# An FFT filter followed by a maxout layer: loads of the opening held behind the first exchange, filter copies and weights on the ACT queue, exchange reads in two t halves, four products on GpSimd

## The chip, the cores and the metric

The kernel runs on one core of one Trainium2 chip. The metric is the device time of one execution in microseconds (us). Every kernel below was run several times. A run counts as slow when its granted TensorE clock (the share of the full clock that the chip allows) is far below the others' or its time is over 1.5% above that kernel's fastest. All medians and ratios below are of fast runs.

Engines in the profile: PE is TensorE (matmul), PEld its weight loads, DVE is VectorE, ACT is ScalarE, POOL is GpSimd, SP is SyncE, which here does nothing but issue DMAs. A trailing q, as in SPq, marks an engine's DMA issues. Such an issue takes place in order: if the next DMA of SP has to wait for data, all DMAs of SP behind it wait too.

## The reference

```python
def _attn_ref(x, filt_r, filt_i):           # x: 8 x 3072 x 256, filters: 1537 x 256
    X = np.fft.rfft(x, axis=1)
    Y = X * (filt_r + 1j * filt_i)[None, :, :]
    return np.fft.irfft(Y, n=x.shape[1], axis=1)

def _moe_ref(x, w1, w2, w_out):             # x: 24576 x 256, hidden size 1024
    return np.maximum(x @ w1, x @ w2) @ w_out
```

The output is the second function of the first one's result, in float32.

## The kernel before

The transform of length 3072 = 128 x 24 is done as two small transforms by matmul, with an exchange through DRAM between them, and the inverse in the same way. For one of the eight batches:

- `gen_f1`: `x` times `C1` gives `at`, stored to DRAM as `ad`, read back rearranged as `bt` (the first exchange).
- `gen_f2`: sixteen groups `g` of two values of `t` each: `px` = `U` times `bt`, one product `pqt` with the filter `F`, then `pz`, stored to DRAM as `zd` and read back rearranged as `zr` (the second exchange).
- `s4`: `py` = `zr` times `G1`; then the maxout layer (`ph`, `po`) in six tiles of 512 tokens, each with one store of output.

```python
# gen_f1, after the last store of ad
for h in range(2):
    for rs in range(4):
        src = ad[32 * rs + 16 * h:32 * rs + 16 * h + 16].rearrange("t n d -> n t d")
        nc.sync.dma_start(out=bt_[24 * rs:24 * rs + 24, 16 * h:16 * h + 16], in_=src)

# gen_f2
def s3(g, pqt):
    ...                                     # pz by four matmuls, zt <- pz on ACT
    if g % 2 == 1:
        nc.sync.dma_start(out=zd[:, 2 * g - 2:2 * g + 2], in_=zt)

for g in list(range(2, 16)) + [0, 1]:
    ...                                     # px by two matmuls
    V.tensor_tensor(pqt, px..., F[:, :, 2 * g:2 * g + 2], OP.mult)
    pend.append((g, pqt))
    if len(pend) > 1:
        s3(*pend.pop(0))
    yield
s3(*pend.pop(0))
zr_ = zrpool.tile([128, N2, D], BF16, tag="zr")
for c in range(3):
    for rs in range(4):
        src = zd[24 * rs + 8 * c:24 * rs + 8 * c + 8].rearrange("n t d -> t n d")
        nc.sync.dma_start(out=zr_[32 * rs:32 * rs + 32, 8 * c:8 * c + 8], in_=src)

# s4, tile i of the batch: four of the 24 columns of zr, all 128 partitions
TE.matmul(py[:, n], zr[b][:, 4 * i + n, 128 * dc:128 * dc + 128], G1, ...)

# the opening
table_c(); load_f(1, 16); load_f(16, 32); uu, mk = tables_u()
drain(gen_f1(0))
copy_f(1, 16); copy_f(16, 32)               # F partitions 48..95 <- 0..47, on SP
load_f0(); load_w()                         # 16 small loads; 2 weights on SP, Wo on Pool
for c in range(12): load_x(1, c)
sines_u(uu, mk); tables_pe()
...                                         # f2 of batch 0, with fix_f before product 14
prep_w(); drain(f2); drain(gen_f1(1)); s4(0)
```

After that one loop interleaves, step by step, the maxout layer of batch b with `gen_f2` of batch b+1 and `gen_f1` of batch b+2.

## Time and profile before

| | before |
|---|---|
| time at the outset, median of 3 runs | 615.84 us (615.23 to 616.15) |
| span of the profiled run | 613.5 us |
| first product `pqt` starts | 55.3 us |
| sixteenth product ends | 82.0 us |
| first `ph` of the maxout layer | 111.7 us |
| first output store | 130.2 us |
| from output store 12 to 18, 18 to 24 and so on (one batch) | 62.7 us |

From the page: the busy time of each engine, then the main DMA queue (packets, MB, share of 16 engines' time).

```profile
PE 536.0 (87%) x4008; PEld 395.0 (64%) x4008; DVE 335.0 (55%) x430; ACT 329.5 (54%) x588; POOL 86.0 (14%) x167
...
q1 hardware_dynamic: 66720, 54.17, 33.6%
```

The next view gives busy time in chosen stretches; the last three columns are the granted TensorE clock, the mean busy share of the DMA engines and what they moved.

```profile
core 0: us, PE busy (x) PEld busy (x) DVE busy (x) ACT busy (x) POOL busy (x), PEclk, DMA share, GB/s
26.00:46.00 20.00, 4.79 (x35) 3.25 (x33) 4.00 (x7) 3.57 (x8) 6.34 (x12) 1.00 1.16 183
234.00:242.00 8.00, 8.00 (x64) 5.69 (x63) 3.25 (x5) 3.92 (x7) 0.54 (x1) 1.00 0.94 260
200.00:300.00 100.00, 100.00 (x784) 75.21 (x783) 61.23 (x73) 61.73 (x111) 14.96 (x28) 1.00 0.71 178
```

From 200 to 300 us TensorE is busy in all of the 100 us. A microsecond taken from another engine is worth nothing there. In the opening (26 to 46 us) it is busy 4.8 of 20 us, while the DMA engines are full. So nearly all the time that can be won lies before about 120 us (a wait of 3.4 us in the second batch, shown below, is the exception).

The timeline of the events that this document follows (start, length, engine and line, output<-input, count; in brackets the idle time before and what ended it):

```profile
27.10 16.50 SPq L318 DMA_DIRECT2D bt__271<-ad  x8
43.72 7.84 SPq L102 DMA_DIRECT2D F<-F  x4
55.27 2.35 DVE L346 TENSOR_TENSOR pqt<-px,F 96x1024 bf16<-96x1024 f32 x2 [23.51 <-DMA F<-F]
76.68 3.02 ACT L335 ACTIVATE zt<-pz 96x512 bf16<-96x512 f32 x6 [11.65 <-DMA zd<-zt]
93.45 10.04 SPq L357 DMA_DIRECT2D zr__665<-zd  x12
108.08 3.05 ACT L310 ACTIVATE at<-pa 128x512 bf16<-128x512 f32 x6 [14.38 <-DMA ad<-at]
...
232.91 7.05 SPq L357 DMA_DIRECT2D zr__2222<-zd  x12
239.89 0.61 PE L369 MATMUL py<-G_59,zr__2222 128*128 128x128 bf16 x8
```

Read it as three waits of the opening: the first product waits for the filter copy, ACT waits 11.6 us for a `zd` store that stands behind small loads on SP, and ACT waits 14.4 us for `ad` stores that stand behind twelve `zr` reads.

The waits of TensorE for the whole run (us in total, times, longest), those that matter here:

```profile
PE px L343 <- DMA bt__271<-ad: 15.3, 1, 15.3
PE py L369 <- ACT at L310: 14.6, 1, 14.6
...
PE px L343 <- DMA bt__1412<-ad: 3.4, 1, 3.4
```

The same view for SP between 200 and 250 us:

```profile
SPq L357 <- DMA zd<-zt: 4.7, 2, 4.2
...
SPq L318 <- DMA ad<-at: 1.7, 1, 1.7
```

### The profile page before, as it was taken

The page shows a single profiled execution, that of the slowest core. Times are in us where ns is not written, and L with a number is a line of the kernel's source. Part 1 is how long each engine was busy: PE and PEld are TensorE (multiplying, and loading weights), DVE is VectorE, ACT ScalarE, POOL GpSimd, SP SyncE. Part 2 cuts the span into 40 slices and gives each one's busy share as a digit, 9 for nine tenths or more (in the row PEclk, how much of TensorE's full clock was granted, in tenths as well). Part 3 has the DMA queues.
Part 4 walks back from the last instruction along what each step waited for, and adds up shares of the span by engine and source line. Part 5 has one row for each costly group of instructions (what it writes and reads, how often), then busy time and mean ns, then how long its engine had stood idle before and what let it go on. Part 6 is the DMA issues. An engine that isn't in the chain of part 4 may idle for free.

```text
span 613.5 us, 10246 instructions
## 1 busy us (share of the span) xinstructions
PE 536.0 (87%) x4008; PEld 395.0 (64%) x4008; DVE 335.0 (55%) x430; ACT 329.5 (54%) x588; POOL 86.0 (14%) x167
## 2 busy tenths in 40 slices
PE   3403771799979999999999999999999999999995
PEld 0203550477657777777777777777777777777774
DVE  8203740288337664666466637663667377734342
ACT  3801161566536754765476556765666455555541
POOL 8430002011111111111121102110000000000000
PEclk9999996699989999999999999999999999999998
DMA  8997529656976596658767785778336822261111
GB/s 140 208 188 148 180 62 219 171 123 169 225 182 156 134 220 198 153 152 183 212 150 179 163 218 145 183 156 233 125 112 161 225 83 78 74 185 70 69 69 69
DMA packets 90784, 94.62 MB, mean 154 GB/s; under 512 B 7360, under 2 KB 71504, under 8 KB 90592
## 3 DMA queue, kind: packets, MB, share of 16 engines
q1 hardware_dynamic: 66720, 54.17, 33.6%
q0 software_dynamic: 24016, 39.81, 28.5%
q8 instruction: 31, 0.51, 0.3%
q14 instruction: 17, 0.14, 0.1%
HBM read 56.72 MB, written 50.33 MB: 174 GB/s over the span
## 4 chain that ended last, share of the span: by engine, by line
PE 43%; issue 34%; DMA 12%; SPq 4%; POOL 3%; ACT 1%; DVE 1%; POOLq 0%; ACTq 0%
PE ph L385 14%; PE po L410 13%; PE po L405 3%; DMA xb<-in_x_dram 3%; PE pz L333 3%; PE px L343 3%; PE pz L334 3%; DMA Wo<-in_moe_w_out_dram 2%; DMA zd<-zt 2%; SPq L117 2%; POOL out_dram L416 2%; PE pa L309 2%; PE py L369 2%; DMA ad<-at 2%; DMA zr__665<-zd 1%
## 5 line engine op out<-in xcount | busy, mean ns | idle before, releaser
L410 PE MATMUL po<-Wo,gt 128*128 128x256 bf16 x1536 | 230.4, 273 | 0.0
L390 ACT ACTIVATE gt<-ph 128x512 bf16<-128x512 f32 x288 | 170.7, 593 | 100.4 <-PE ph L385 97.0
L346 DVE TENSOR_TENSOR pqt<-px,F 96x1024 bf16<-96x1024 f32 x128 | 156.0, 1219 | 107.6 <-PE px L343 83.6
L410 PEld LDWEIGHTS <-gt 128*128 128x128 bf16 x1536 | 150.2, 98 | 58.2
L335 ACT ACTIVATE zt<-pz 96x512 bf16<-96x512 f32 x128 | 75.3, 593 | 111.4 <-PE pz L334 87.9
L412 DVE COPY ot<-po 128x512 f32<-128x512 f32 x96 | 66.4, 692 | 75.8 <-PE po L410 75.8
L416 POOL DMA_DIRECT2D out_dram<-ot x48 | 25.8, 537 | 452.9 <-DVE ot L412 418.1
L385 PEld LDWEIGHTS <-Wd 128*128 128x128 bf16 x768 | 74.0, 99 | 19.5 <-issue 4.8
L310 ACT ACTIVATE at<-pa 128x512 bf16<-128x512 f32 x96 | 55.8, 597 | 54.0 <-PE pa L309 33.9
L388 DVE TENSOR_SCALAR gt<-ph 128x512 bf16<-128x512 f32 x96 | 65.5, 682 | 28.7 <-PE ph L385 28.7
L333 PE MATMUL pz<-pqt,VP 96*96 96x256 bf16 x256 | 67.9, 289 | 11.0 <-DVE pqt L346 10.7
L334 PE MATMUL pz<-pqt,VQ 96*96 96x256 bf16 x256 | 68.2, 290 | 0.0
L87 POOL DMA_DIRECT2D xb<-in_x_dram x96 | 51.4, 558 | 66.4 <-PE pa L309 50.4
L343 PEld LDWEIGHTS <-U 96*96 96x96 bf16 x256 | 32.5, 134 | 24.6 <-issue 22.9
L309 PE MATMUL pa<-xb,C_58 128*128 128x512 bf16 x96 | 38.3, 409 | 10.3 <-DMA xb<-in_x_dram 9.4
L334 PEld LDWEIGHTS <-VQ 96*96 96x96 bf16 x256 | 33.4, 130 | 13.2 <-issue 12.7
L333 PEld LDWEIGHTS <-VP 96*96 96x96 bf16 x256 | 33.7, 131 | 1.8 <-DVE pqt L346 1.1
L343 PE MATMUL px<-bt__271,U 96*96 96x256 bf16 x32 | 9.8, 416 | 18.3 <-DMA bt__271<-ad 15.3
L309 PEld LDWEIGHTS <-C_58 128*128 128x128 bf16 x96 | 9.5, 99 | 18.3 <-issue 7.5
L369 PE MATMUL py<-G_59,zr__665 128*128 128x128 bf16 x48 | 4.6, 248 | 14.6 <-ACT at L310 14.6
L369 PEld LDWEIGHTS <-zr__665 128*128 128x128 bf16 x48 | 3.9, 112 | 15.9 <-DMA zr__665<-zd 9.8
L374 DVE TENSOR_SCALAR y__760<-py 128x512 bf16<-128x512 f32 x1 | 0.7, 692 | 19.9 <-PE py L369 19.9
(334 smaller groups left out, 565.8 us busy)
## 6 DMA issues: line engine op xcount, KB each, us to landing
out_dram<-ot POOLq DMA_DIRECT2D x48, 512.0 KB, 3.9
xb<-in_x_dram POOLq DMA_DIRECT2D x96, 128.0 KB, 6.0
ad<-at SPq DMA_DIRECT2D x48, 256.0 KB
zd<-zt SPq DMA_DIRECT2D x64, 192.0 KB
bt__271<-ad SPq DMA_DIRECT2D x8, 192.0 KB
zr__665<-zd SPq DMA_DIRECT2D x12, 128.0 KB
bt__727<-ad SPq DMA_DIRECT2D x8, 192.0 KB
zr__1295<-zd SPq DMA_DIRECT2D x12, 128.0 KB
```

The source lines that it names most:

```text
L309: TE.matmul(pa, C1, xb[b, c], start=True, stop=True)
L310: S.activation(at[:, 2 * (c % 2):2 * (c % 2) + 2], pa, AF.Copy)
L333: TE.matmul(pz[:, i], VP[:, 2 * g + i], pqt[:, 0, i], start=True, stop=False)
L334: TE.matmul(pz[:, i], VQ[:, 2 * g + i], pqt[:, 1, i], start=False, stop=True)
L335: S.activation(zt[:, 2 * (g % 2):2 * (g % 2) + 2], pz, AF.Copy)
L343: TE.matmul(px[:, i], U[:, 2 * g + i].rearrange("p a b -> p (a b)"), bt_[:, 2 * g + i], start=True, stop=True)
L346: V.tensor_tensor(pqt, px.rearrange("p (o i) d -> p o i d", o=1).to_broadcast([QP, 2, 2, D]), F[:, :, 2 * g:2 * g + 2], OP.mult)
L385: TE.matmul(ph, Wd[:, dc, 128 * j:128 * j + 128], y_[:, dc].rearrange("p a b -> p (a b)"), start=(dc == 0), stop=(dc == 1))
L388: V.tensor_scalar(gt[tt][:, j], ph, 0.0, None, OP.max)
L390: S.activation(gt[tt][:, j], ph, AF.Relu)
L410: TE.matmul(p_, g_[:, jj, 128 * n:128 * n + 128], Wo[:, jj], start=False, stop=(jj == 7))
L412: V.tensor_copy(ot[tt][:, n - 1:n + 1], po[tt])
```

## The change

The intent is to shorten the opening in four ways.

1. Loads that the first product does not need (`x` of the next batch, `Wo`) are held until after products; F0 comes in four loads and a copy.
2. The filter copies and the two weight loads go from SP to the ACT queue, so they no longer stand behind the exchange reads.
3. The groups start with `t` 16 to 31, and `zr` is read in two halves of `t`: the upper half as soon as its eight groups are done, the lower one at the end. This holds for all eight batches.
4. In batch 0, Pool takes four of the sixteen products.

```diff
+    zrpool = ctx.enter_context(tc.tile_pool(name="zrpool", bufs=2))
 ... (cut: the tile pool of zr leaves its later place)
     def copy_f(t0, t1):
         for ri in range(2):
-            nc.sync.dma_start(out=F[48:96, ri, t0:t1], in_=F[0:48, ri, t0:t1])
+            S.dma_start(out=F[48:96, ri, t0:t1], in_=F[0:48, ri, t0:t1])
 ... (cut: F0 in four loads on SP, then copy_f0, two DMAs on ACT)
     def load_w():
-        nc.sync.dma_start(out=w1f, ...)
-        nc.sync.dma_start(out=w2f, ...)
+        S.dma_start(out=w1f, ...)
+        S.dma_start(out=w2f, ...)
+
+    def load_wo():
         G.dma_start(out=Wo, ...)
 ... (cut; in s3, after the store of zd)
+            if g == 15:
+                zr[b] = zrpool.tile([128, N2, D], BF16, tag="zr", name="zr")
+                read_z(1)
+            if g == 1:
+                read_z(0)
+
+        def read_z(h):
+            for rs in range(4):
+                src = zd[24 * rs:24 * rs + 24, 16 * h:16 * h + 16].rearrange("n t d -> t n d")
+                nc.sync.dma_start(out=zr[b][32 * rs + 16 * h:32 * rs + 16 * h + 16], in_=src)
-        for g in list(range(2, 16)) + [0, 1]:
+        for n, g in enumerate(list(range(8, 16)) + list(range(2, 8)) + [0, 1]):
 ...
-            V.tensor_tensor(pqt, px..., F[:, :, 2 * g:2 * g + 2], OP.mult)
+            E = V
+            if b == 0 and n in (1, 5, 9, 12):
+                E = G
+                xs = init.tile([QP, 2, D], FP32, tag="xs", name="xs")
+                S.activation(xs, px, AF.Copy)
+                px = xs
+            E.tensor_tensor(pqt, px..., F[:, :, 2 * g:2 * g + 2], OP.mult)
 ... (cut: the twelve zr reads at the end of gen_f2 go)
+    load_f0()
     table_c()
+    load_f(16, 32)
     load_f(1, 16)
-    load_f(16, 32)
     uu, mk = tables_u()
     drain(gen_f1(0))
-    copy_f(1, 16)
-    copy_f(16, 32)
-    load_f0()
-    load_w()
-    for c in range(12):
-        load_x(1, c)
     sines_u(uu, mk)
     tables_pe()
+    copy_f(16, 32)
+    copy_f(1, 16)
+    copy_f0()
+    load_w()
 ... (cut: fix_f one product later)
+        if n == 1:
+            load_wo()
+        for c in range(12):
+            if n == (1, 5, 9)[c // 4]:
+                load_x(1, c)
+    drain(f2)
     prep_w()
 ...
-    drain(f2)
     drain(gen_f1(1))
```

The loop over `h` in the `bt` reads is not touched. It still reads `t` 0 to 15 first, while the groups now begin with `t` 16.

More of the change, by code (lines that the diff above doesn't have):

```diff
@@ L109, in load_f0, with copy_f0 @@
             for dr in range(2):
-                for mm, row0 in enumerate((0, 96) if dr == 0 else (32, 64)):
-                    for q in range(2):
-                        p0 = 48 * q + 24 * dr + mm
-                        if p0 == 48:
-                            nc.sync.dma_start(out=F0[48:49, ri], in_=f[1536:1537, :])
-                            nc.sync.dma_start(out=F0[50:72:2, ri], in_=fsrc(f, 128, 128, J - 1, 1, 1))
-                        else:
-                            nc.sync.dma_start(out=F0[p0:p0 + 23:2, ri], in_=fsrc(f, row0, 128, J, 1, 1))
+                src = bass.AP(f.tensor, f.offset + 32 * dr * D, [[128 * D, J], [(96 - 64 * dr) * D, 2], [1, D]])
+                nc.sync.dma_start(out=F0[24 * dr:24 * dr + 24, ri], in_=src)
+    def copy_f0():
+        S.dma_start(out=F0[48:96], in_=F0[0:48])
+        S.dma_start(out=F0[48:49, 0], in_=filt_r[1536:1537, :])
     SW = init.tile([QP, QP], BF16)
@@ L275, in load_w @@
     def load_w():
-        nc.sync.dma_start(out=w1f, in_=moe_w1.rearrange("(c p) j -> p c j", p=128))
-        nc.sync.dma_start(out=w2f, in_=moe_w2.rearrange("(c p) j -> p c j", p=128))
+        S.dma_start(out=w1f, in_=moe_w1.rearrange("(c p) j -> p c j", p=128))
+        S.dma_start(out=w2f, in_=moe_w2.rearrange("(c p) j -> p c j", p=128))
+    def load_wo():
         G.dma_start(out=Wo, in_=moe_w_out.rearrange("(c p) j -> p c j", p=128))
@@ L345, in gen_f2 @@
             pqt = pqpool.tile([QP, 2, 2, D], BF16, tag="pq")
-            V.tensor_tensor(pqt, px.rearrange("p (o i) d -> p o i d", o=1).to_broadcast([QP, 2, 2, D]),
+            E = V
[4 more added lines that the diff above has]
+                px = xs
+            E.tensor_tensor(pqt, px.rearrange("p (o i) d -> p o i d", o=1).to_broadcast([QP, 2, 2, D]),
                             F[:, :, 2 * g:2 * g + 2], OP.mult)
@@ L352, in gen_f2 @@
         s3(*pend.pop(0))
-        zr_ = zrpool.tile([128, N2, D], BF16, tag="zr")
-        for c in range(3):
-            for rs in range(4):
-                src = zd[24 * rs + 8 * c:24 * rs + 8 * c + 8].rearrange("n t d -> t n d")
-                nc.sync.dma_start(out=zr_[32 * rs:32 * rs + 32, 8 * c:8 * c + 8], in_=src)
-        zr[b] = zr_
         yield
@@ L421, in drain @@
             pass
+    load_f0()
     table_c()
+    load_f(16, 32)
     load_f(1, 16)
-    load_f(16, 32)
     uu, mk = tables_u()
     drain(gen_f1(0))
-    copy_f(1, 16)
-    copy_f(16, 32)
-    load_f0()
-    load_w()
-    for c in range(12):
-        load_x(1, c)
     sines_u(uu, mk)
     tables_pe()
+    copy_f(16, 32)
+    copy_f(1, 16)
+    copy_f0()
+    load_w()
     f2 = gen_f2(0)
-    for g in range(16):
-        if g == 13:
+    for n in range(16):
+        if n == 14:
             fix_f()
         next(f2)
+        if n == 1:
[4 more added lines that the diff above has]
+    drain(f2)
     prep_w()
     setup.close()
-    zrpool = ctx.enter_context(tc.tile_pool(name="zrpool", bufs=2))
     ypool = ctx.enter_context(tc.tile_pool(name="ypool", bufs=3))
```

## The prediction

> **What bounds the kernel now.** Matrix work saturates TensorE from about 120 us on (20.0 of every 20 us busy in the stretch table from 200 us), so only the opening can give time back. The first maxout matmul (`ph`) starts at 111.7 us. The chain of waits up to there is mostly DMA and SP issues. The timeline gives three blocks:
>
> 1. To 55.3 us: the first product waits for the filter copy F<-F. The DMA engines are busy throughout (mostly 150 to 260 GB/s). The exchange reads `bt` are issued from 27.1 us but land at 46, because the next batch's `x` and the output weight share the engines; the filter copies leave SP only after them (43.7 to 51.6).
> 2. 55.3 to 81.9: sixteen products, one each 1.37 us (VectorE 1.22), plus a stall of about 4 us: the store of `zt` stands on SP behind 16 small issues of F0 (0.7 us each), so ACT waits 11.6 us.
> 3. 81.9 to 111.7: weight preparation (7 us) ahead of the last product, last store of `zd` at 93.2, twelve `zr` reads issued over 10 us, and ACT waiting 14.4 us for stores of `ad` held behind them.
>
> **What the change does.**
>
> Block 1: moves 2.1 MB (as written) of other loads behind the exchange, and only half of the filter copy has to be there for the first product. 9.8 MB before the first product become about 7.0; at the 190 GB/s of this stretch that is 15 us less. The `bt` reads still start near 27. First product about 40 us. [...]
>
> Block 2: the 4 us stall goes. Pool's four products I expect to cost, not to save: TensorE is in order and only one product is pending, so a Pool product holds up everything two steps on. [...] Block 2 stays near 29 us.
>
> Block 3: the last product no longer waits for weight preparation, half of `zr` is read earlier, and four reads instead of twelve stand before the `ad` stores. From 30 us to about 17.
>
> First `ph` near 86 us: 26 less, all on the critical path because TensorE is saturated afterwards. In the second batch the 3.4 us stall at 174.5 us (reads `bt` behind twelve `zr` issues) should shrink by about 2, less what it costs that products now begin with the half read last. Later batches: nothing.
>
> **Prediction.** 615.8 - 26 - 1 = 589 us; 8 in 10 between 579 and 599. Faster by over 2%: 0.95; within 2%: 0.04; slower: 0.01.
>
> **What would show each step.** The timeline: first product at 38 to 44 us instead of 55.3; `bt` landed by 40; [...] no ACT wait on `zd` over 3 us; first `ph` at 82 to 92; TensorE busy shares after 200 us as before, and 62.7 us per batch.
>
> **What would make it wrong.** DMAs from ACT taking the engines from `bt` (`bt` took 19 us beside `x`), so the first product stays near 48. [...] ACT held long in its issues.

Some passages of the prediction are cut, because no trace or run shows what they say, or none did when it was written: how long ACT's copies would be held, how long a product takes on Pool, and what was reckoned from that. The sum came to 40 + 29 + 17 = 86 us for the first `ph`, 26 less than 111.7, and with 1 us of the second batch to 615.8 - 26 - 1 = 589. The price of Pool's products was a term of the 29.

Two statements can be read in the traces. The loads that share the engines with `bt`: from 27 to 46 us of the kernel before, the queue of Pool, with `x` and `Wo`, moved 2.55 MB and that of SP 0.92 (the first `px` starts at 46.05; the last `bt` packets end at 51.5). TensorE in order: in the changed kernel it stands idle for 1.66 us up to 59.51, when a Pool product is done, and the next `px`, whose `bt` had landed at 47.5, starts only behind that product's `pz`, at 60.32.

## More of the kernel before

Note the destination of a `zr` read: 32 neighbouring partitions. In units of one read, a third `c` of the columns comes in four reads.

## The result, and the profile after

| | before | after |
|---|---|---|
| median of the runs of this comparison | 615.54 us (614.37 to 616.15, 4 runs) | 658.63 us (658.24 to 659.58, 4 runs) |
| ratio after / before | | 1.0705 [1.0684, 1.0726] |
| span of the profiled run | 613.5 | 656.5 |
| first product | 55.3 | 49.0 |
| sixteenth product ends | 82.0 | 76.4 |
| first `ph` | 111.7 | 103.2 |
| first output store | 130.2 | 124.1 |
| output store 12 to 18 | 62.7 | 71.0 |

Ratios are the mean time of one kernel's fast runs over that of the other's fast runs of the same rounds, so they are not quite the ratio of the medians quoted; brackets are 95% intervals.

The kernel became 7% slower. The opening did get shorter, but every batch except the last got longer.

```profile
PE 541.8 (83%) x3939; PEld 399.0 (61%) x4008; DVE 330.5 (50%) x426; ACT 332.3 (51%) x592; POOL 94.8 (14%) x171
...
q1 hardware_dynamic: 65168, 50.44, 42.1%
```

Some matmul records are missing in this trace (3939 against 4008 weight loads), so batches are told by the output stores. The line to look at is q1 (a packet is one piece of a transfer as the trace records it; in the reads of `bt` and `zr` it is a row of 512 B): the SP queue moved fewer packets and fewer bytes than before (the copies and weights went to the ACT queue), yet its packets took 42.1% of a longer span instead of 33.6%. Its packets had become slower.

```profile
213.00:221.00 8.00, 7.95 (x62) 6.11 (x62) 5.43 (x8) 4.75 (x10) 1.60 (x3) 1.00 1.17 101
240.00:248.00 8.00, 3.11 (x23) 1.97 (x21) 1.38 (x2) 1.46 (x3) 0.00 (x0) 0.86 1.11 101
200.00:300.00 100.00, 92.59 (x713) 70.30 (x725) 59.50 (x69) 57.92 (x105) 14.44 (x27) 0.97 0.82 160
```

The columns are those of the table of stretches before. The two stretches of 8 us are those of the two half reads. The DMA engines are fully busy in them and yet move 101 GB/s, nearly all of it `zr`, against 260 (175 of it `zr`) in the stretch of the whole read before. And in the last row TensorE has lost 7.4 of 100 us.

```profile
26.10 8.08 SPq L319 DMA_DIRECT2D bt__278<-ad  x8
29.74 6.70 ACTq L103 DMA_DIRECT2D F<-F  x4
49.03 1.22 DVE L363 TENSOR_TENSOR pqt<-px,F 96x1024 bf16<-96x1024 f32 x1 [17.49 <-PE px L354]
50.13 2.12 POOL L363 TENSOR_TENSOR pqt<-xs,F 96x1024 bf16<-96x1024 f32 x1 [32.20 <-ACT xs L361]
82.25 1.08 ACT L336 ACTIVATE zt<-pz 96x512 bf16<-96x512 f32 x2 [6.90 <-DMA zd<-zt]
98.04 1.08 ACT L311 ACTIVATE at<-pa 128x512 bf16<-128x512 f32 x2 [5.08 <-DMA ad<-at]
...
212.55 1.84 SPq L348 DMA_DIRECT2D zr<-zd  x4
239.24 1.99 SPq L348 DMA_DIRECT2D zr<-zd  x4
249.66 1.01 PE L380 MATMUL py<-G_59,zr 128*128 128x128 bf16 x8 [6.55 <-DMA zr<-zd]
```

The last line has a wait that did not exist before: `py` waits 6.55 us for `zr`. It starts 10.4 us after the issue of the second half (before: 7.0 us after the issue of the first third). The waits of TensorE over the whole run:

```profile
PE py L380 <- DMA zr<-zd: 29.3, 5, 6.5
PE px L354 <- DMA bt__278<-ad: 17.8, 1, 17.8
...
PE px L354 <- DMA bt__1400<-ad: 11.2, 1, 11.2
```

And of SP between 200 and 250 us, to be set beside 4.7 and 1.7 us before:

```profile
SPq L348 <- DMA zd<-zt: 10.4, 3, 5.1
SPq L319 <- DMA ad<-at: 6.9, 1, 6.9
```

The chain of waits of this batch shows how the parts join (start, length, piece):

```profile
233.23 5.92 DMA zd<-zt
...
240.71 8.59 DMA zr<-zd
...
249.66 1.01 PE py L380 x8
```

So one batch runs like this. The first half read is issued at 212.5 us and keeps the DMA engines busy until 221.4. The last stores of `ad`, issued at 214.5 and 217.3 us, stand behind it: packets of such stores (2,048 B) appear only from 220.4 us. So SP waits 6.9 us for them before it can issue the `bt` reads (at 224.65). The last `zd` stores stand behind these on SP. The second half can be issued only when they have landed, takes 8.6 us from its last issue, and `py` needs all of it. Measured from the end of the last product of this batch (224.3 us before, 227.4 after), the reads are issued 3.2 us later than they were (11.8 instead of 8.6) and `py` starts another 3.4 us later after that (10.4 instead of 7.0). That is the wait. On top of it comes the clock: in stretches of 2 us the granted clock is 0.50 from 246 to 252 us, and full again from 254. It fell at 245.7 us, 2.6 us after the last matmul, and came back at 252.5, 2.9 us after the first `py`. The wait of 6.5 us, and about 1.4 us for the 2.9 us of work at a clock of 0.50 (an estimate, half of the 2.9; five `po` matmuls took 1.27 us there and 0.71 at the full clock), make 8.0 us; the batch lost 8.1.

For each group of `zr` reads, the packets of 512 B in the trace were counted out:

```
before: 12 reads  issued 232.9   packets 32 ns   233.9 to 242.8 (9.0 us), 1.57 MB
after:   4 reads  issued 212.6   packets 94 ns   213.5 to 221.4 (7.9 us), 0.79 MB
         4 reads  issued 239.2   packets 91 ns   240.2 to 248.4 (8.2 us), 0.79 MB
```

Half the bytes take nearly the time of the whole. A packet of the same size takes three times as long. Over all sixteen groups of the changed kernel the mean packet took 61 to 94 ns (median 88); over the eight whole reads of the kernel before, 30 to 38.

### The profile page after: what moved, and what is told of

Its sections match the earlier page's. It is cut to its first block, busy times and chain, and to the rows that moved or that the text cites. A ratio compares the mean times of both kernels' runs of the same rounds, so it can differ in the third digit from the quotient of the medians.

```text
span 656.5 us, 10072 instructions
## 1 busy us (share of the span) xinstructions
PE 541.8 (83%) x3939; PEld 399.0 (61%) x4008; DVE 330.5 (50%) x426; ACT 332.3 (51%) x592; POOL 94.8 (14%) x171
## 3 DMA queue, kind: packets, MB, share of 16 engines
q1 hardware_dynamic: 65168, 50.44, 42.1%
## 4 chain that ended last, share of the span: by engine, by line
PE 38%; issue 34%; DMA 18%; POOL 4%; SPq 3%; ACT 2%; DVE 1%; POOLq 0%; ACTq 0%
PE po L421 11%; PE ph L396 10%; DMA zd<-zt 5%; DMA zr<-zd 4%; DMA ad<-at 4%; PE pz L334 3%; PE px L354 3%; PE pz L335 3%; PE po L416 3%; DMA bt__278<-ad 2%; SPq L319 2%; PE pa L310 2%; POOL out_dram L427 2%; PE py L380 2%; DMA bt__1400<-ad 1%
## 5 line engine op out<-in xcount | busy, mean ns | idle before, releaser
L421 PE MATMUL po<-Wo,gt 128*128 128x256 bf16 x1536 | 233.9, 276 | 3.0 <-issue 1.1
L363 DVE TENSOR_TENSOR pqt<-px,F 96x1024 bf16<-96x1024 f32 x124 | 151.2, 1220 | 120.2 <-PE px L354 120.1
L421 PEld LDWEIGHTS <-gt 128*128 128x128 bf16 x1536 | 151.9, 99 | 61.3 <-issue 3.3
L423 DVE COPY ot<-po 128x512 f32<-128x512 f32 x96 | 66.4, 692 | 81.1 <-PE po L421 81.1
L396 PEld LDWEIGHTS <-Wd 128*128 128x128 bf16 x768 | 75.2, 100 | 23.1 <-issue 7.9
L380 PE MATMUL py<-G_59,zr 128*128 128x128 bf16 x384 | 32.0, 231 | 34.6 <-DMA zr<-zd 29.3
L380 PEld LDWEIGHTS <-zr 128*128 128x128 bf16 x384 | 27.2, 103 | 37.8 <-issue 37.1
L335 PEld LDWEIGHTS <-VQ 96*96 96x96 bf16 x256 | 33.6, 131 | 8.5 <-issue 8.2
L354 PE MATMUL px<-bt__278,U 96*96 96x256 bf16 x32 | 9.9, 419 | 17.8 <-DMA bt__278<-ad 17.8
L310 PEld LDWEIGHTS <-C_58 128*128 128x128 bf16 x96 | 9.5, 99 | 17.8 <-issue 7.5
L354 PE MATMUL px<-bt__1400,U 96*96 96x256 bf16 x32 | 6.4, 281 | 11.2 <-DMA bt__1400<-ad 11.2
```

The source lines that it names most:

```text
L310: TE.matmul(pa, C1, xb[b, c], start=True, stop=True)
L335: TE.matmul(pz[:, i], VQ[:, 2 * g + i], pqt[:, 1, i], start=False, stop=True)
L354: TE.matmul(px[:, i], U[:, 2 * g + i].rearrange("p a b -> p (a b)"), bt_[:, 2 * g + i], start=True, stop=True)
L363: E.tensor_tensor(pqt, px.rearrange("p (o i) d -> p o i d", o=1).to_broadcast([QP, 2, 2, D]), F[:, :, 2 * g:2 * g + 2], OP.mult)
L396: TE.matmul(ph, Wd[:, dc, 128 * j:128 * j + 128], y_[:, dc].rearrange("p a b -> p (a b)"), start=(dc == 0), stop=(dc == 1))
L421: TE.matmul(p_, g_[:, jj, 128 * n:128 * n + 128], Wo[:, jj], start=False, stop=(jj == 7))
```

## Theories

**Partitions.** A half read writes 16 neighbouring partitions, a read of before 32. The packets of the half reads took 61 to 94 ns, those of before 30 to 38. The theory is that the choice of the written partitions sets these times. Why it should, no trace of this case shows.

**Rivals.** (a) The order of the groups is at fault, because `bt` is still read in the old order. (b) The source is: a half row of `zd` is read with a longer stride. (c) Pool's products are. (d) The copies on the ACT queue are.

## The experiments

The first four runs shared one chip (before: 613.9 us), the next four another (611.7), the last four a third (613.6). For each run the table has the first product, the end of the sixteenth, the first `ph`, the first output store, then the time from output store 0 to 6, 6 to 12 and so on (one batch each), all from its profile. That is one execution each, and executions differ: after, e1 and e12 are alike up to the first product, which comes at 49.0, 48.9 and 46.8 us, and after and e12 are alike up to the first `ph` (103.2 and 99.4). A single difference of 2 to 4 us in the opening therefore means little. The profiled run of e2 was the slowest of its four, that of e6 the fastest by 5 us. There is no row for e9. All outputs are right.

| run | 1st product | 16th ends | first `ph` | 1st store | batches |
|---|---|---|---|---|---|
| before | 55.3 | 82.0 | 111.7 | 130.2 | 72.5 62.7 62.7 62.7 62.7 61.2 55.3 |
| after | 49.0 | 76.4 | 103.2 | 124.1 | 81.6 70.8 71.0 71.4 71.6 67.3 55.3 |
| e1_zr_whole | 48.9 | 76.3 | 96.8 | 119.6 | 78.3 62.7 62.7 62.7 62.7 61.2 55.3 |
| e2_zr_spread | 47.3 | 74.6 | 95.8 | 117.9 | 75.3 66.6 64.9 63.8 64.7 61.2 55.3 |
| e3_before_halves | 58.1 | 83.1 | 119.7 | 139.8 | 81.1 70.6 70.6 72.0 71.9 69.8 55.6 |
| e4_no_pool | 58.1 | 82.1 | 105.8 | 128.1 | 82.2 72.5 72.0 71.4 71.7 70.8 55.9 |
| e5_pool_one | 47.1 | 70.0 | 94.3 | 116.3 | 75.2 64.6 64.4 63.9 63.4 61.2 55.3 |
| e6_half_first | 42.8 | 73.9 | 94.4 | 112.4 | 68.6 64.0 62.7 62.7 63.5 61.2 55.3 |
| e7_copies_sp | 43.7 | 72.1 | 93.6 | 116.1 | 72.7 66.6 64.8 63.8 65.4 61.2 55.3 |
| e8_all_three | 42.4 | 69.3 | 94.5 | 112.6 | 68.6 63.8 65.2 64.5 64.2 61.2 55.3 |
| e10_act_free | 42.7 | 66.0 | 91.6 | 109.0 | 71.3 63.1 62.7 62.7 62.7 61.2 55.3 |
| e11_wide_whole | 43.2 | 66.0 | 92.9 | 111.5 | 69.8 62.7 63.8 62.7 62.7 61.2 55.3 |
| e12_halves_b0 | 46.8 | 74.1 | 99.4 | 121.8 | 77.7 62.8 62.7 62.7 62.7 61.2 55.3 |

The sum closes: after gained 6.1 us up to the first store and lost 9.1 + 8.1 + 8.3 + 8.7 + 8.9 + 6.1 = 49.2 us in the batches, 43.1 in all; the spans differ by 43.0. The batches carry it, so a spread of 2 to 4 us in the opening does not touch this.

### e1_zr_whole: the halves undone, all else kept

```diff
-            if g == 15: ... read_z(1)
-            if g == 1:  read_z(0)
+        # at the end of gen_f2, as before
+        for c in range(3):
+            for rs in range(4):
+                nc.sync.dma_start(out=zr[b][32 * rs:32 * rs + 32, 8 * c:8 * c + 8], in_=...)
```

> The changed kernel with only the reads of zr put back as before (twelve reads of 32 partitions after the last store). Theory (the two-half reads of zr, each written to 16 partitions, are slow, 91 ns a packet against 32 to 38, and hold up the SP queue in every batch): batches go back to 62.7 us, no TensorE wait for zr after 200 us, first ph near 97 us, in all about 600 us. Rival (the loss comes from the new order of the groups, whose first products need the half of bt that is read last): still 8 us lost per batch, 645 us or more.

Measured: 609.97 us (608.49 to 610.82), ratio 0.9929 [0.9884, 0.9975]. The later batches are back at 62.7 us, and TensorE is again busy in all of the 100 us from 200 on (columns as before):

```profile
200.00:300.00 100.00, 100.00 (x788) 75.18 (x787) 60.12 (x73) 61.33 (x110) 12.87 (x25) 1.00 0.76 184
```

So the halves are the cause of the loss there, and the order of the groups, which this run keeps, is not. The total is 10 us above what the theory expected, because the first batch still takes 78.3 us: TensorE waits 3.3 and 9.4 us for `bt` of the second and third batch. That is the order's share, taken up by e6. The longer of the two:

```profile
PE px L344 <- DMA bt__1408<-ad: 9.4, 1, 9.4
```

### e2_zr_spread: the halves kept, their partitions spread

The reads, their source, number and time stay; each writes every fourth partition of one half of the 128. `C1` is permuted to match before it becomes `G1`.

```diff
-  out=zr[b][32 * rs + 16 * h:32 * rs + 16 * h + 16]
+  out=zr[b][64 * h + rs:64 * h + rs + 61:4]
```

> The changed kernel with both half reads kept, source side untouched, but the 16 partitions of a read are every fourth one instead of 16 in a row (the columns of C1 are permuted for G1, so the result stays right). Theory [...]: packets of zr near 45 ns, a half in about 4 us instead of 8, stalls gone, about 595 us. Rival source [...]: packets stay near 91 ns and the time near 655 us.

The mechanisms named for theory and rival are cut, as no trace or run shows them. The 45 ns and 4 us are about half of the 91 ns and 8 us measured in the changed kernel.

Measured: 610.36 us (606.65 to 614.92), ratio 0.9942 [0.9865, 1.0018]. In the quickest of its sixteen groups a half now takes 4.1 us (0.79 MB, so 192 GB/s) and its packets 43 ns instead of 91 to 94. Over all groups it is 4.1 to 7.3 us and 32 to 46 ns (median 42).

```profile
201.00:206.00 5.00, 5.00 (x39) 3.71 (x37) 3.22 (x5) 3.40 (x7) 1.02 (x2) 1.00 0.95 179
```

The row, with the columns of the tables of stretches above, is one half read: 179 GB/s over the stretch instead of 101, with TensorE busy throughout. Since the source is what it was, rival (b) falls. Which partitions are written decides. The halves still cost 1 to 4 us per batch: TensorE waits for `zr` 6.8 us in all (four times, 2.0 at most), presumably because the first `py` needs both halves complete and not only a third; e10, with whole reads, has 0.2 us of this wait. The time is 15 us above the expected 595: these waits and those for `bt` (2.5 and 4.9 us) were not in it.

### e3_before_halves: the kernel before, with the new order and the halves alone

```diff
 # on the kernel before
-        for g in list(range(2, 16)) + [0, 1]:
+        for g in list(range(8, 16)) + list(range(2, 8)) + [0, 1]:
+            ... read_z(1) at g == 15, read_z(0) at g == 1
```

> The kernel before with one part of the change alone: order of the groups and reads of zr in two halves. Theory (this part alone makes the loss): 8 us lost per batch, 650 to 665 us. Rival (loss needs the rest of the change too, loads on the ACT queue or Pool): below 625 us.

Measured: 676.6 us (676.25 to 678.78), ratio 1.1026 [1.0965, 1.1086]. Without any other part of the change, the later batches take 70.6 to 72.0 us and `zr` waits add up to 31.7 us. Rivals (c) and (d) can't explain the batches. The first `ph` comes 8 us later than in the kernel before, and the first batch takes 81.1 us instead of 72.5; with that the time lies above the 650 to 665 that were expected.

### e4_no_pool: all products on VectorE

```diff
-            if b == 0 and n in (1, 5, 9, 12):
+            if False:
```

> The changed kernel with all products on VectorE. Theory (a Pool product of 2.1 us plus its ACT copy holds the in-order TensorE up, about 1.4 us each): the sixteen products of the first batch take 22 to 23 us instead of 27.4; in all up to 5 us less (650 to 655), less if the slow half read of zr swallows it. Rival (Pool relieves VectorE): the products take longer and the time rises by up to 3 us.

Measured: 663.56 us (661.88 to 669.97), ratio 1.0824 [1.0752, 1.0896]. The later batches stay slow (71.4 to 72.5), which again acquits Pool. The expected 650 to 655 us did not come: the sixteen products did take less (24.0 us instead of 27.4), but they began 9 us later. So the run doesn't tell the price of Pool's products, since it changed a second thing: without a product on Pool, nothing holds Pool's loads back.

```profile
18.30 0.91 POOL L279 DMA_DIRECT2D Wo<-in_moe_w_out_dram  x1
```

`Wo` was issued at 18.3 us instead of 52.2, `x` of the next batch followed, and the first product came at 58.1 instead of 49.0 us. In the changed kernel, "held behind the exchange" works only because Pool executes in order and its first product waits for the exchange.

### e5_pool_one: e2 with one product on Pool

```diff
 # on e2
-            if b == 0 and n in (1, 5, 9, 12):
+            if b == 0 and n == 1:
```

> The spread kernel (half reads of zr on every fourth partition) with only the first of the four Pool products kept, because that one also holds the weight and x loads back in Pool's order; the other three go to VectorE. Theory (each Pool product costs 1.4 to 1.8 us in the in-order TensorE loop): the sixteen products take 23 to 24 us instead of 27.3, first ph 3 to 4 us earlier than 95.8, time 0 to 4 us below the spread kernel. Rival (Pool helps): products take 28 us or more.

Measured: 607.11 us in its three fast runs (602.61 to 609.62; the fourth, at 611.86, counts as slow), ratio 0.9909 [0.9857, 0.996]. The gate is kept, three products go back. The sixteen products take 22.9 us (47.1 to 70.0) instead of 27.3 (47.3 to 74.6): 1.5 us per product of Pool. Of these 4.4 us only 1.5 arrive at the first `ph`, which is within the spread of single executions; TensorE then waits 7.0 us for the weight preparation (3.3 in e2).

### e6_half_first: e2 with the half that is needed first read first

```diff
 # on e2, in the bt reads of gen_f1
-                for h in range(2):
+                for h in (1, 0):
```

> The spread kernel with the two halves of the bt reads swapped, so that the half which the new order of the groups needs first is also read first. Theory (the swapped order makes the first product wait for all of bt): first product 38 to 44 us instead of 47.3 (then the filter copies decide), waits of TensorE for bt in the second and third batch (2.5 and 4.9 us) gone, time 8 to 14 us below the spread kernel. Rival (the DMA engines are saturated and the order does not matter): first product at 46 to 48, time as the spread kernel.

Measured: 601.27 us (595.64 to 602.75), ratio 0.9807 [0.9761, 0.9853]. The first `px` comes at 36.1 instead of 46.6 us, the first product at 42.8; what it waits for is now the filter copy:

```profile
36.12 1.06 PE L356 MATMUL px<-bt__278,U 96*96 96x256 bf16 x4 [5.40 <-DMA bt__278<-ad]
42.80 1.22 DVE L365 TENSOR_TENSOR pqt<-px,F 96x1024 bf16<-96x1024 f32 x1 [11.12 <-DMA F<-F]
```

The first batch falls from 75.3 to 68.6 us, and the waits for `bt` of the second and third batch are gone from the list. So rival (a) is right as a second, separate cause: an order that was changed at the consumer and not at the producer.

### e7_copies_sp: e2 with the filter copies back on SP

```diff
 # on e2
-            S.dma_start(out=F[48:96, ri, t0:t1], ...)
+            nc.sync.dma_start(out=F[48:96, ri, t0:t1], ...)   # behind the bt reads
 # load_w() moved behind the second product
```

> The spread kernel with the filter copies back on SP behind the bt reads and the two weight loads on ACT moved behind the first products, so that bt has the engines alone. Theory (the copies on ACT take the engines from bt): packets of bt 40 ns instead of 54, all of bt there by 38 to 40 us instead of 45.7, but the copies land after it, so the first product still comes at 44 to 48 and the time stays within 3 us of the spread kernel. Rival (the copies don't touch bt): bt complete at 45 to 47 as before.

Measured: 608.94 us (605.76 to 611.06), ratio 0.9945 [0.9908, 0.9982]. All of `bt` has landed at 39.6 us instead of 45.7 in e2, and the first product starts at 43.7 instead of 47.3. The packets of `bt` took 49 ns against 54; I had expected 40, so the size of this effect was missed, not its direction. The DMAs that ACT and SP issue do run interleaved: in the trace of the changed kernel 192 packets of the copies (7,680 and 8,192 B, 564 and 727 ns each) lie among the 3,072 of `bt` (55 ns each). That is 7.7 us of all 16 engines beside 10.6. In its later batches, without such copies, `bt` packets took 35 to 41 ns. The copies are not all of it, as the 49 ns of e7 were measured with most of them behind the `bt` reads.

### e8_all_three: e2, e5 and e6 together

> Spread writes of zr, first half of bt read in the order of use, one Pool product instead of four: the version the experiments point to. If the three costs are independent: first ph near 84 to 88 us, no TensorE wait for zr or bt over 2 us, 590 to 598 us (3 to 4% faster than before). If the time won in the opening turns into waits for DMA in the second and third batch: 603 to 608.

Measured: 599.8 us (598.11 to 602.32), ratio 0.9803 [0.9772, 0.9835]. It fell between the two ranges that were expected and can't be told from e6 (601.27). The products end 4.6 us earlier than in e6 (69.3 against 73.9), but the first `ph` is no earlier (94.5 against 94.4), and the halves still cost 6.1 us of waits for `zr`.

### e9_whole_first: e1 with the half order of e6 and one Pool product

> The changed kernel with zr read whole after the last store as before (twelve reads of 32 partitions), bt read in the order of use, one Pool product. In the kernel before the first y of a batch needs only the first third of zr (4 of 12 reads); with halves it needs all eight. Theory (so even fast halves cost waits in the steady batches, 1 to 2 us each): no TensorE wait for zr or bt over 1 us after the opening, every later batch 62.7 us, first ph near 94, time 592 to 597 and steady from run to run. Rival (the waits of the spread kernels come from elsewhere): 598 to 604 as the spread kernel with all three.

Measured: 593.02 us in its three fast runs (591.79 to 594.03), ratio 0.9655 [0.9613, 0.9697]. With the whole read in place of the halves the opening's gain is kept to the end, and the kernel is faster than the one before by over 3%.

### e10_act_free: e9, the small copies and weights on SP

```diff
 # on e9
-        S.dma_start(out=F0[48:96], ...)      # and F0[48:49], w1f, w2f
+        nc.sync.dma_start(out=F0[48:96], ...)
```

> The kernel of the run above with the small F0 copies and the two weight loads issued on SP instead of ACT. Theory (ACT stands from 37 to 45 us in its own DMA issues, which wait for the F0 copy to land, so the Pool product's copy and the first zt come 4 us after the first product): the sixteen products start at 42 to 43 and end 3 to 4 us earlier than in the run above, first ph and time 2 to 4 us less (589 to 594). Rival (the ACT queue costs nothing): within 1 us of the run above.

The 37 to 45 us can be read in e6: ACT issues the F0 copy at 37.05 us and the load behind it at 45.44.

Measured: 593.18 us (590.33 to 593.49), ratio 0.9649 [0.961, 0.9688], not told apart from e9. The products end at 66.0 us and the first `ph` is the earliest of those in the table, but the 2 to 4 us that I expected did not come. The timeline shows why:

```profile
72.36 5.89 SPq L364 DMA_DIRECT2D zr<-zd  x12
78.36 13.03 SPq L313 DMA_DIRECT2D ad<-at  x6
...
88.55 1.07 PE L375 MATMUL py<-G,zr 128*128 128x128 bf16 x8 [10.10 <-ACT at L311]
```

The twelve reads stand before the stores of `ad` on SP, ACT waits for these with its buffers, and `py` waits 10.1 us for ACT. This is block 3 of the prediction once more, and whatever is won before it is lost in it. This version beats both kernels; together with e9 it is the best.

### e11_wide_whole: e10, whole reads on every fourth partition

```diff
 # on e10, C1 permuted as in e2
-  out=zr[b][32 * rs:32 * rs + 32, 8 * c:8 * c + 8]
+  out=zr[b][rs:rs + 125:4, 8 * c:8 * c + 8]
```

> The kernel of the run above with the 32 partitions of each whole read of zr spread over every fourth partition. Theory (packet time follows from how widely the written partitions lie): packets of zr below those of 32 neighbouring partitions (32 to 38 ns), down to 25 to 30; no gain in time because whole reads already arrive before they are needed. Rival (something else sets the packets now): 32 to 38 ns as before.

Measured: 596.25 us (595.14 to 599.65), ratio 0.9718 [0.9675, 0.9762]. The packets took 27 to 29 ns in steady batches, against 34 to 38 in e10. So the packet times, each the mean of one group of reads, can be compared for four choices of partitions:

| partitions written by one read | run | ns per packet of 512 B, all groups of the run |
|---|---|---|
| 16 neighbours | after | 61 to 94, median 88 |
| 16, every fourth | e2 | 32 to 46, median 42 |
| 32 neighbours | before, e10 | 30 to 38, median 34 |
| 32, every fourth | e11 | 27 to 31, median 28 |

But nothing was gained in time (it is 3 us slower than e10, in all four runs, for which no cause was sought): a whole `zr` took 8.9 us instead of 9.2, since its twelve reads are issued one after another, here over 8.5 us, and TensorE has no wait for `zr` to lose. Spread alone does not order the table: 16 partitions, every fourth, have a higher median (42) than 32 neighbours (34), though the two ranges overlap.

### e12_halves_b0: the changed kernel with halves in batch 0 alone

```diff
-            if g == 15:
+            if b == 0 and g == 15:
 # (the same for g == 1; whole reads for b > 0)
```

> The changed kernel with half reads of zr in the first batch alone, whole reads in the other seven. Accounting of the loss: theory (the steady batches carry it, the opening about 6 us of it): first ph near 103 as in the changed kernel, batches after the third 62.7 us, time about 616 (610 of the run with whole reads plus 6). Rival (the opening's half reads carry more, by shifting all that follows): 625 or more.

Measured: 614.2 us (612.23 to 616.37), ratio 1.0013 [0.9969, 1.0058]. The later batches are at 62.7 us. So the halves of the seven later batches carry the loss from 1.0013 to 1.0705, and those of batch 0, which the change was meant to help, perhaps cost a little too (e1, without them: 0.9929; the intervals of the two ratios just touch).

## Why the prediction was wrong

I predicted 589 us, faster with a chance of 0.95. It came to 658.6, slower by 7%.

1. **"Later batches: nothing."** This is the step that failed. Measured: 8.1 to 8.9 us lost in each of batches two to five, 49.2 us in all. The prediction looked at the halves only in the opening and counted them as "four reads instead of twelve". It did not ask what one of the new reads costs (16 partitions at 101 GB/s), nor that a half is of no use to `py` until the other is there, while a third of the columns serves two of the six tiles. It also took "TensorE is saturated" as if slack of the DMA chain were without limit. e1, e3 and e12 show that the halves did it, e2 that the partitions they write did most of it.
2. **Block 3, "from 30 us to about 17".** Measured: 26.8 us (76.4 to 103.2), from the same cause: in e1 it is 20.5 us, with the twelve reads (in e12, with the halves, 25.3). ACT waited 6.9 us for a store of `zd`, where at most 3 was predicted. The other part, ACT waiting for stores of `ad`, remains in every version.
3. **Block 1, "first product about 40 us".** Measured: 49.0. Holding the loads back did work, but the second half of `bt`, all of which landed only at 47.5 us, is the half that the new order wants first; the lower half was complete at 32.9. With the reads turned round (e6) the first product is at 42.8, in the range predicted of 38 to 44. The named risk, copies on ACT beside `bt`, is real as well: 3.6 us in e7, which moved the weights too. Its stated outcome, a first product that "stays near 48", is what came (49.0), though either repair alone, e6 or e7, ends it.
4. **The second batch, a stall "should shrink by about 2, less what it costs that products now begin with the half read last".** It grew from 3.4 to 11.2 us. The cost was named and left out of the sum. e1 still has 9.4 + 3.3 us of it, e6 none.
5. **Block 2, "near 29 us", and products on Pool "to cost, not to save".** Measured 27.4 us; a Pool product took 2.12 us after 0.59 of copy. The sign held: a Pool product costs 1.5 us (e5).
6. **The opening's size on its own.** Even without the halves (e1) the kernel is at 609.97 us, above the range of 579 to 599. With the half order and one Pool product as well (e9) it is at 593.0. That is near the 589 predicted, but partly by luck: e9 has given up the third part of the change and most of the fourth, so it does not confirm the sum term by term.

What stays open: the runs show that the partitions written decide (e2 against after: medians of 42 and 88 ns), and the table of e11 gives the times for four choices of them. They don't show why, nor why e2's packets (median 42 ns) are slower than those of before (34). The price of the Pool gate alone was not measured, as e4 confounded it. The last wait of e10 was shown and no cure for it was tried.

## What to carry to other kernels

Cost a DMA also by the partitions it writes, not by its bytes and its count alone: here, cutting a read into slices of 16 neighbouring partitions made each byte nearly twice as slow (in the batch shown 16.1 us, 7.9 and 8.2, for the two halves against 9.0 for the whole), while the reads of before, cut along the columns, give `py` a usable first part. When a change to the opening lies in code that every iteration runs, cost it in the steady state too, and count how much slack its chain of stores and reads has before TensorE waits. When the order of use changes, change the order of the reads with it, and when loads are "held back", find out what holds them: here it was one product that stands before them on Pool.
